# Batch 0's values in rows of 512 bytes, ordered by TensorE, in a fused windowed attention and GELU block

## The chip, the core and the metric

The kernel runs on one core of a Trainium2 chip. Its engines are TensorE (PE, matmuls into PSUM), VectorE (DVE), ScalarE (ACT), GpSimd (POOL) and SyncE (SP, which here only issues transfers); each takes its instructions in order, and they wait for each other by semaphores. The metric is the device time of one execution in microseconds, as the median of several runs. Times inside a run come from one profiled execution.

## The reference

Eight batches of 576 tokens, eight heads of 64. Each token attends to those within 32 places of it; the heads' outputs side by side are the tokens of a two-layer network with GELU (tanh form). All inputs and the output are float32.

```python
scores = np.matmul(q, k.transpose(0, 1, 3, 2)) / np.sqrt(64)          # 8 x 8 x 576 x 576
scores = np.where(np.abs(pos[:, None] - pos[None, :]) <= 32, scores, -1e9)
attn = np.exp(scores - max); attn = attn / (attn.sum(-1) + 1e-9)
x = np.matmul(attn, v).transpose(0, 2, 1, 3).reshape(4608, 512)
out = gelu_tanh(x @ moe_w_in) @ moe_w_out                             # 512 x 2048, 2048 x 512
```

## The kernel before

The 4608 tokens go through the network in nine tiles of 512. Attention of batch t+1 is woven into the second product of tile t, by plans written by hand (`PLAN_0`, `PLAN_1`, `PLAN`); the order of all instructions of an engine is the order of the program. Only batch 0 has nothing to hide in: its attention is the kernel's beginning, and this is where the change lies.

**Layouts.** The 512 first queries and keys of a batch are loaded with four rows to a partition (row 4p + j in partition p, `qk`, L144), cast to fp16, and turned by TensorE for each of four pairs of heads (`trans_pair`, L378). `trans_out` copies the result out of PSUM: queries stay ordered by (j, p), keys are put back in natural order (L390), so that 64 neighbouring keys are one block. Each pair's `score` (L447) multiplies key blocks with the queries that can see them. For batch 0 the mask is added first, by four matmuls of an identity block `idn` with prepared tiles `bias` (L457); every key row of a block must thus stand in the order that `bias` has. The sum of the exponentials comes from a matmul with `ones` (`sum_up`, L495), its inverse from ACT's Ln and Exp (`invert`, L530 and L531). `times` (L505) multiplies the values, 16 matmuls for a pair; `spread` (L540) scales the result on DVE into `xT`, whose four slices are the contraction dimension of the first product, pair g being slice g.

The values `V` hold 128 natural rows to a chunk: slots 0 to 3 are the chunks, slots 4 to 6 hold the blocks shifted by 64, made from the chunks by two DVE copies (`pair_v`, L225 and L226). A pair's values come by two transfers, one for each head, in rows of one token, 256 bytes (`v_of_pair`, L271); POOL casts them into V (`values`, L844; DVE for the last pair).

**The first product.** Tile 0 has 16 column blocks of 128 (`ffn_in`, L577). Each adds four matmuls, dc 0 to 3, one for each slice of `w_in` and of `xT`. `block_in(ns, *dcs)` issues them slice by slice over several columns: six columns first (`six`), then two, six and two. `w_in` comes in eight transfers of 512 KB (`load_w_in`, L246): x is the half of its columns, dc the slice; `cast_w_in` (L250) casts each in two halves, on two engines.

**Order of loads on SP before**: q and k of batch 0 (the first k and one q from ACT's queue) with the keys' tails; the tails of V (`vt`); pairs 0, 1 and 2 of V; w_in dc 0; head 6 of V; w_in dc 1; head 7; w_in dc 2, dc 3, then its other half; then batch 1's q and k and w_out, in turns. Loads share eight semaphores, so each waits for the landing of the load eight before it.

**Order on TensorE before**, from the third score on: score of pair 2, turning of pair 3's q and k, sum of pair 1, score of pair 3, sum of pair 2, `times` 0 and 1, two spins (matmuls with no use but to keep TensorE running), sum 3, two spins, `times` 2, then dc 0 and dc 1 of six columns, `times` 3, dc 2 and dc 3.

Of the kernel before, what the change touches and what calls it, by code (L numbers as in the profile page):

```python
# [78 lines left out]
def kernel(  # L79
# [9 lines left out]
    nc = tc.nc  # L89
# [36 lines left out]
    band = const.tile([128, 4, 144], FP16, name="band")  # L126
    KTs = [const.tile([128, NPAIR, 512], FP16, name=f"KT{i}") for i in range(2)]
# [9 lines left out]
    def load_early(b):  # L137
# [12 lines left out]
        def vs(*cs):  # L150
            if len(raws[b]) < 4:
                raws[b].append(stage.tile([128, 4, H, 64], FP32, name="vr", tag="stage"))
                raws[b].append(tailp.tile([128, 4, 64], FP32, name="vt", tag="vt"))
# [115 lines left out]
    def v_of_pair(g, hs=(0, 1)):  # L269
        for h in (2 * g + x for x in hs):  # L270
            nc.sync.dma_start(raws[0][3][:, :, h, :], v[0, h, 0:512, :].rearrange("(c p) d -> p c d", p=128))  # L271

    vs(4)
    for g in range(3):
        v_of_pair(g)
    for x in range(2):
        load_w_in(0, x)
        v_of_pair(3, (x,))
# [23 lines left out]

    def blocks(copy, dst, src, r, *pieces):
# [14 lines left out]
    nc.vector.memset(ones, 1.0)  # L318

# [58 lines left out]
    def trans_pair(b, pr, pt, ptk=None, now=True, copy=nc.vector.tensor_copy):  # L378
# [4 lines left out]
        for j in range(4):  # L383
            nc.tensor.transpose(ptk[:, j, :], k16[:, pr, j, :, :], idn)
# [3 lines left out]
    def trans_out(b, pr, pt, ptk, copy=nc.vector.tensor_copy):  # L388
        nc.vector.tensor_copy(QTs[b][:, pr, :, 0:128], pt[:, 0:4, :])
        copy(  # L390
            KTs[b % 2][:, pr, :].rearrange("d (p j) -> d p j", j=4),
            ptk[:, 0:4, :].rearrange("d j p -> d p j"))
# [47 lines left out]
    def work_of(b, g):  # L440
# [4 lines left out]
        return (band[:, :, p0:144], range(NPAIR), TAIL if b else TAIL_0, [(7, p0, 144)], p0, 144 - p0)  # L445

    def score(b, g, pair):  # L447
# [5 lines left out]
        if added:  # L453
            for half in range(2):
                for h in range(2):
                    r0 = 64 * h
# [353 lines left out]
    def sums_of(g):  # L810
        d = pieces("DO"[g % 2], "ps_d")
        sum_up(0, g, d, groups[(0, g)])
        lts[g] = invert(0, g, d)
# [9 lines left out]
    score(0, 0, 0)  # L823
    turn(1)
# [8 lines left out]
    cast_vt(0)  # L833
# [5 lines left out]
    score(0, 3, 1)  # L839
    sums_of(2)  # L840

    def values(g, copy):
        hs = slice(2 * g, 2 * g + 2)
        copy(Vs[0][:, 0:4, hs, :], raws[0][3][:, :, hs, :])  # L844
        pair_v(0, nc.vector.tensor_copy, hs)
# [5 lines left out]
    values(0, nc.gpsimd.tensor_copy)  # L851
# [258 lines left out]
```

## Time and profile before

| what | us |
|---|---|
| median of three runs (lowest, highest) | 297.86 (296.98, 298.21) |
| the profiled execution | 299.54 |
| its span from first to last instruction | 297.8 |
| busy in the span: PE, DVE, ACT, POOL | 285.9, 212.8, 196.4, 89.3 |
| busy from 0 to 20 us: PE, DVE, ACT, POOL | 15.65, 11.06, 13.23, 7.76 |
| start of dc 0, dc 1, dc 2 of the first product | 18.03, 20.43, 22.49 |
| start of its casts of w_in on POOL (x = 0, dc 0 to 3) | 16.88, 19.76, 21.82, 23.02 |

Lines of the timeline read: start, duration (both in us), engine and line, operation, output <- input, shape, count; in brackets the idle time of that engine just before, and what ended it. Where a row has a count above one, its duration spans all of them. Lines of windows read, for each engine, busy microseconds and, in brackets, the number of instructions that started; then the granted TensorE clock, the mean busy share of the 16 transfer engines, and the GB/s that they moved. Lines of the chain read start, duration, who.

### The profile page before, as it was taken

What the parts mean: (1) busy time and instruction counts of PE and PEld (TensorE: products, weight loads), DVE (VectorE), ACT (ScalarE), POOL (GpSimd) and SP (SyncE); (2) the same over time, 40 slices, a digit from 0 to 9 for tenths busy, and PEclk for the clock granted to TensorE, in tenths of its full rate; (3) what the DMA queues carried; (4) which work ended last, traced back from release to release, by engine and by line L of the source; (5) the groups of instructions that cost most, each with busy time, mean ns of one, the idle gap of its engine ahead of it and who ended that gap; (6) DMA issues with size and microseconds to landing.
All of it is one profiled execution on the core that took longest, in us unless ns stands there. A gap on an engine that the chain in (4) does not pass through costs nothing.

```text
span 297.8 us, 7286 instructions
## 1 busy us (share of the span) xinstructions
PE 285.9 (96%) x2945; PEld 192.6 (65%) x2945; DVE 212.8 (71%) x467; ACT 196.4 (66%) x315; POOL 89.3 (30%) x143
## 2 busy tenths in 40 slices
PE   7879999999999999999999999999999999999992
PEld 3434544557875687568855885588557867877781
DVE  4655378897897667868786878686857867865852
ACT  5965766778577875777667765786578558707700
POOL 3426315102347622305260615060800050024000
PEclk9999999999999999999999999999999999999999
DMA  7999999999999996999988999999693040013013
GB/s 231 235 327 412 353 310 221 257 183 193 268 240 195 262 219 130 146 130 242 163 191 132 251 117 191 111 244 155 118 147 42 2 130 12 2 36 109 0 55 89
DMA packets 114392, 51.02 MB, mean 171 GB/s; under 512 B 98471, under 2 KB 110247, under 8 KB 114102
## 3 DMA queue, kind: packets, MB, share of 16 engines
q1 hardware_dynamic: 89460, 38.67, 61.4%
q0 software_dynamic: 23776, 10.83, 23.3%
q10 hardware_dynamic: 1122, 1.06, 1.1%
q8 instruction: 23, 0.38, 0.6%
q14 instruction: 11, 0.09, 0.1%
HBM read 36.70 MB, written 9.44 MB: 155 GB/s over the span
## 4 chain that ended last, share of the span: by engine, by line
PE 85%; DMA 6%; SPq 3%; DVE 2%; ACT 1%; issue 0%; POOL 0%; ACTq 0%
PE mm L751 33%; PE ph L577 17%; PE mm L577 17%; PE ps_s L468 3%; PE pu L629 3%; DMA wst<-in_moe_w_in_dram 2%; PE ps_d L495 2%; DMA KT<-k 2%; PE mm L723 2%; PE py L723 2%; PE ps_o L505 2%; SPq L271 2%; DMA qr<-in_q_dram 1%; PE mm L629 1%; PE ps_od L495 1%; SPq L246 1%
## 5 line engine op out<-in xcount | busy, mean ns | idle before, releaser
L577 PEld LDWEIGHTS <-w_in 128*128 128x128 f16 x512 | 57.4, 113 | 50.4 <-POOL w_in L250 2.1
L577 PE MATMUL ph<-xT,w_in 128*128 128x512 f16 x256 | 64.6, 379 | 1.1 <-POOL w_in L250 1.1
L577 PE MATMUL mm<-xT,w_in 128*128 128x512 f16 x256 | 64.1, 379 | 0.0
L713 POOL DMA_DIRECT2D out_dram<-y x55 | 32.3, 597 | 84.9 <-DVE y L780 76.2
L585 ACT ACTIVATE gT<-mm 128x512 f16<-128x512 f32 x60 | 35.6, 598 | 33.1 <-PE mm L577 32.5
L751 PEld LDWEIGHTS <-s 128*128 128x128 f16 x512 | 49.3, 98 | 7.1 <-DVE s L694 0.6
L751 PE MATMUL mm<-t,s 128*128 128x256 f16 x376 | 45.2, 273 | 0.2 <-DVE y L764 0.2
L694 DVE TENSOR_TENSOR s<-gT 128x512 f16<-128x512 f16 x64 | 27.8, 435 | 19.4 <-ACT gT L585 19.3
L751 PEld LDWEIGHTS <-gT 128*128 128x128 f16 x384 | 36.2, 98 | 6.4
L585 ACT ACTIVATE gT<-ph 128x512 f16<-128x512 f32 x58 | 32.4, 604 | 11.2 <-PE ph L577 11.2
L481 ACT ACTIVATE pe<-ps_s 128x960 f16<-128x960 f32 (+1 forms) x31 | 29.6, 976 | 13.4 <-PE ps_s L468 13.3
L751 PE MATMUL mm<-w_out,gT 128*128 128x256 f16 x256 | 32.6, 273 | 0.0
L104 ACT ACT_TABLE_LOAD x18 | 23.1, 1283 | 2.2 <-issue 1.9
L530 ACT ACTIVATE lt<-ps_d 128x480 f32<-128x480 f32 (+2 forms) x28 | 15.5, 555 | 11.4 <-PE ps_d L495 7.9
L531 ACT ACTIVATE lt<-lt 128x480 f32<-128x480 f32 (+3 forms) x36 | 21.1, 586 | 1.1
L490 DVE TENSOR_TENSOR pe<-pe,band 128x960 f16<-128x960 f16 x28 | 18.1, 664 | 2.1 <-ACT pe L481 2.0
L505 PEld LDWEIGHTS <-V 128*64 128x64 f16 x520 | 13.8, 111 | 6.4 <-DVE V L226 1.6
L751 PE MATMUL mm<-t,gT 128*128 128x256 f16 x128 | 16.2, 273 | 0.0
L216 POOL DMA_DIRECT2D V<-in_v_dram x16 | 14.4, 910 | 1.3 <-POOL after L989 0.4
L694 DVE TENSOR_TENSOR s<-s,gT 128x512 f16<-128x512 f16 x32 | 13.9, 435 | 1.1
L751 PE MATMUL mm<-w_out,s 128*128 128x256 f16 x120 | 14.6, 273 | 0.0
L540 DVE TENSOR_TENSOR xT<-ps_o,lt 128x480 f16<-128x480 f32 (+5 forms) x26 | 13.4, 535 | 1.6 <-ACT w_in L250 1.1
(149 smaller groups left out, 390.7 us busy)
## 6 DMA issues: line engine op xcount, KB each, us to landing
kr<-in_k_dram SPq DMA_DIRECT2D x31, 256.0 KB, 9.7
qr<-in_q_dram SPq DMA_DIRECT2D x6, 1024.0 KB, 6.1
wst<-in_moe_w_in_dram SPq DMA_DIRECT2D x8, 512.0 KB, 7.4
wst<-in_moe_w_out_dram SPq DMA_DIRECT2D x2, 1024.0 KB, 10.6
wst<-in_moe_w_out_dram SPq DMA_DIRECT2D x4, 512.0 KB, 7.5
qr<-in_v_dram SPq DMA_DIRECT2D x8, 256.0 KB, 6.9
V<-in_v_dram POOLq DMA_DIRECT2D x16, 128.0 KB, 8.5
qr<-in_q_dram SPq DMA_DIRECT2D x7, 256.0 KB, 7.3
```

What stands on the lines that cost most here:

```text
L104: nc.scalar.add_instruction(mybir.InstLoadActFuncSet(name=nc.get_next_instruction_name(), act_func_set_id=which, ins=[], outs=[]))
L216: nc.gpsimd.dma_start(V[:, c, :, :], v[b, :, 128 * c:128 * c + 128, :].rearrange("h p d -> p h d"))
L481: nc.scalar.activation(pe, ps[:, :, 0:w], AF.Exp, scale=SCALE)
L490: nc.vector.tensor_tensor(pe, pe, m.rearrange("k (o j) p -> k o j p", o=1).broadcast_to(list(pe.shape)), op=ALU.mult)
L505: nc.tensor.matmul(o[64 * h:64 * h + 64, cols].rearrange("d (j p) -> d j p", j=4)[:, :, p0 - q0:p1 - q0], Vs[b % 2][:, slot, 2 * pr + h, : ...
L530: nc.scalar.activation(lt[:, 0:n], d[:, 0:n], AF.Ln)
L531: nc.scalar.activation(lt[:, 0:n], lt[:, 0:n], AF.Exp, scale=-1.0)
L577: nc.tensor.matmul(ph, w_cols[:, dc, fc // 4, fc % 4, :], xT[:, dc, t * 512 % RING:t * 512 % RING + 512], start=(dc == 0), stop=(dc == 3))
L585: nc.scalar.activation(gTs[t][:, fc, :], phs[fc], AF.Gelu_apprx_tanh)
L694: nc.vector.tensor_tensor(dst, x, y, op=op)
L713: eng.dma_start(out_v[b, j, q0 + p:q0 + p + e, cols], yo[m:m + e, cols])
L751: nc.tensor.matmul(pys["apart"][:, 0:256] if apart else py[:, blk, :], lhsT, wino[w][:, f, :], start=(new and i % (8 if one else 16) == 0) ...
```

## The change

Three things in the beginning of the kernel, all for batch 0 alone.

- *Values.* A pair's two transfers now split by rows instead of heads: 256 rows each, two rows to a partition, so that 512 bytes are contiguous. Partition p of half c holds rows 256c + 2p and 2p + 1, which is no chunk of 128 rows. Each pair is cast on POOL into a scratch tile (`v16` in `pad`, which lies in the place of the first tile's `gT`), eight matmuls with 32 columns of a permutation matrix `pick` bring the rows to the partitions where they belong (`turn_pair`), DVE copies the result from PSUM into V (`place_pair`), and `pair_v` follows as before. On SP the order becomes: pair 0, `vt`, pair 1, w_in dc 0, pairs 2 and 3, w_in dc 1, dc 2 and so on.
- *Keys.* `pick` leaves the 64 rows of a block in another order than the natural one, so the keys take the same order: the copy out of PSUM writes them by blocks (`trans_out`), and the mask is added through a permuted identity block (`in_block`), with the natural one for the last eight columns: six matmuls instead of four for each score. The mask that the tail of batch 0 is multiplied with gets its own tile `band_0`, one half of it made by a matmul and an ACT copy.
- *Order.* The four spins go. On TensorE, after the sum of pair 1: turning of V 0, score 3, turning of V 1, sum 2, `times` 0, sum 3, turning of V 2, `times` 1, turning of V 3, dc 0 of six columns, dc 1 of three, `times` 2, dc 1 of the other three, dc 2 of three, `times` 3, dc 2 of the other three, dc 3. On POOL: casts of V 0, `vt`, V 1, V 2, half of w_in dc 0, V 3, then halves of w_in. On DVE: place and pair copies of V 0 and 1, scaling of 0 and 1, place and pair copies of V 2, place of V 3, scaling of 2, pair copies of 3, scaling of 3, half of w_in dc 3, then the copies of `band`. On ACT the other half of w_in dc 0 stands between the inverses of sums 2 and 3.

```diff
+    band_0 = const.tile([128, 4, 16], FP16, name="band_0")
...
-                raws[b].append(stage.tile([128, 4, H, 64], FP32, name="vr", tag="stage"))
+                raws[b].append(stage.tile([128, 4, H, 64] if b else [128, 2, H, 128], FP32, name="vr", tag="stage"))
...
-    def v_of_pair(g, hs=(0, 1)):
-        for h in (2 * g + x for x in hs):
-            nc.sync.dma_start(raws[0][3][:, :, h, :], v[0, h, 0:512, :].rearrange("(c p) d -> p c d", p=128))
-
+    def v_of_pair(g):
+        if len(raws[0]) < 4:
+            vs()
+        for c in range(2):
+            nc.sync.dma_start(raws[0][3][:, c, 2 * g:2 * g + 2, :],
+                              v[0, 2 * g:2 * g + 2, 256 * c:256 * c + 256, :].rearrange("h (p j) d -> p h (j d)", j=2))
+
+    v_of_pair(0)
     vs(4)
-    for g in range(3):
-        v_of_pair(g)
-    for x in range(2):
-        load_w_in(0, x)
-        v_of_pair(3, (x,))
+    v_of_pair(1)
+    load_w_in(0, 0)
+    v_of_pair(2)
+    v_of_pair(3)
+    load_w_in(0, 1)
...
+    pad = gp.tile([128, NF, 512], FP16, name="gT", tag="gT")
+    v16 = pad[:, 0:4, :].rearrange("p g (c h x) -> p g c h x", c=2, h=2)
+    pick = pad[:, 4, 0:128]
+    def in_block(r):
+        return pad[r, 4, 384:448]
+    nc.gpsimd.tensor_copy(pick.rearrange("p (q y a) -> p q y a", q=4, y=2),
+                          idn.rearrange("p (q a y) -> p q y a", q=4, y=2))
+    for r in (even, odd):
+        nc.gpsimd.tensor_copy(in_block(r).rearrange("k (x y a) -> k x y a", x=2, y=2),
+                              idn[r, r].rearrange("k (a y x) -> k x y a", x=2, y=2))
...
+    nc.gpsimd.tensor_copy(band_0[even, :, :], full[even, :, 16:32])
...
-            nc.tensor.transpose(ptk[:, j, :], k16[:, pr, j, :, :], idn)
+            nc.tensor.transpose(ptk[:, j if b else (0, 2, 1, 3)[j], :], k16[:, pr, j, :, :], idn)
...
+        if b == 0:
+            copy(KTs[0][:, pr, :].rearrange("d (b j p) -> d j b p", b=8, j=4),
+                 ptk[:, 0:4, :].rearrange("d j (b p) -> d j b p", b=8))
+        else:
...
-                    nc.tensor.matmul(sides[h][64 * half:64 * half + 64, :], idn[r0:r0 + 64, r0:r0 + 64],
-                                     bias[half][r0:r0 + 64, :, :], start=True, stop=False,
-                                     skip_group_check=True)
+                    for by, cols in (((in_block(r), slice(0, 128)),) if half else
+                                     ((in_block(r), slice(0, 120)), (idn[r, r], slice(120, 128)))):
+                        nc.tensor.matmul(side[:, :, cols], by, bias[half][r, :, cols], start=(cols.start == 0),
+                                         stop=False, skip_group_check=True)
...
+    def cast_pair(g, copy):
+        copy(v16[:, g, :, :, :], raws[0][3][:, :, 2 * g:2 * g + 2, :])
+    def turn_pair(g, ps):
+        at = ps.rearrange("k (c y h d) -> k y c h d", c=2, y=2, h=2)
+        for y in range(2):
+            for half in range(2):
+                for j in range(2):
+                    p0, q0 = 64 * half + 32 * j, 64 * y + 32 * half
+                    nc.tensor.matmul(at[p0:p0 + 32, y, :, :, :], pick[:, q0:q0 + 32],
+                                     v16[:, g, :, :, 64 * j:64 * j + 64], start=True, stop=True)
+    def place_pair(g, ps):
+        nc.vector.tensor_copy(Vs[0][:, 0:4, 2 * g:2 * g + 2, :],
+                              ps.rearrange("k (c h d) -> k c h d", c=4, h=2))
...
-    finish(0, bank(0))
-    finish(1, bank(1))
-    s0 = psS.tile([128, 2, 512], FP32, name="ps_o", tag="S0")
-    spin(2, 512, s0[:, 1, :])
-    sums_of(3)
-    spin(2, 512, s0[:, 1, :])
-    values(2, nc.gpsimd.tensor_copy)
+    cast_pair(0, nc.gpsimd.tensor_copy)
+    cast_vt(0)
+    at0 = psO.tile([128, 512], FP32, name="ps_v", tag="D")
+    turn_pair(0, at0)
+    score(0, 3, 1)
+    place_pair(0, at0)
+    pair_of(0, nc.vector.tensor_copy)
+    cast_pair(1, nc.gpsimd.tensor_copy)
+    at1 = psM.tile([128, 512], FP32, name="ps_v", tag="x1")
+    turn_pair(1, at1)
+    sums_of(2)
+    place_pair(1, at1)
+    pair_of(1, nc.vector.tensor_copy)
+    finish(0, bank(0))
+    cast_pair(2, nc.gpsimd.tensor_copy)
+    nc.gpsimd.tensor_copy(w_in16[:, 0, 0:512], wi[0, 0][:, 0, 0:512])
+    cast_pair(3, nc.gpsimd.tensor_copy)
+    sums_of(3, nc.scalar.copy)
+    at23 = psS.tile([128, 2, 512], FP32, name="ps_v", tag="S1")
+    turn_pair(2, at23[:, 0, :])
+    finish(1, bank(1))
+    turn_pair(3, at23[:, 1, :])
+    place_pair(2, at23[:, 0, :])
+    pair_of(2, nc.vector.tensor_copy)
+    place_pair(3, at23[:, 1, :])
...
-    cast_w_in(0, 0, nc.gpsimd.tensor_copy, nc.scalar.copy)
-    values(3, nc.vector.tensor_copy)
-    block_in(six, 0)
+    block_in((4, 5, 0, 2, 3, 1), 0)
     cast_w_in(0, 1, nc.gpsimd.tensor_copy, nc.scalar.copy)
-    block_in(six, 1)
+    block_in((0, 2, 3), 1)
+    finish(2, s1[:, 0, :])
+    pair_of(3, nc.vector.tensor_copy)
+    block_in((1, 4, 5), 1)
+    cast_w_in(0, 2, nc.gpsimd.tensor_copy, nc.scalar.copy)
+    load_table(gelu_set)
+    block_in((0, 1, 2), 2)
     finish(3, s1[:, 1, :])
-    load_table(gelu_set)
-    cast_w_in(0, 2, nc.gpsimd.tensor_copy, nc.scalar.copy)
+    block_in((3, 4, 5), 2)
     cast_w_in(0, 3, nc.gpsimd.tensor_copy, nc.vector.tensor_copy)
-    block_in(six, 2, 3)
+    block_in(six, 3)
```

More of the change, by code (lines that the diff above doesn't have):

```diff
@@ L389, in trans_out @@
         nc.vector.tensor_copy(QTs[b][:, pr, :, 0:128], pt[:, 0:4, :])
-        copy(
-            KTs[b % 2][:, pr, :].rearrange("d (p j) -> d p j", j=4),
-            ptk[:, 0:4, :].rearrange("d j p -> d p j"))
+        if b == 0:
+            copy(KTs[0][:, pr, :].rearrange("d (b j p) -> d j b p", b=8, j=4),
+                 ptk[:, 0:4, :].rearrange("d j (b p) -> d j b p", b=8))
+        else:
+            copy(
+                KTs[b % 2][:, pr, :].rearrange("d (p j) -> d p j", j=4),
+                ptk[:, 0:4, :].rearrange("d j p -> d p j"))
     def bank(i):
@@ L444, in work_of @@
         p0 = cut(b)
-        return (band[:, :, p0:144], range(NPAIR), TAIL if b else TAIL_0, [(7, p0, 144)], p0, 144 - p0)
+        return (band[:, :, p0:144] if b else band_0, range(NPAIR), TAIL if b else TAIL_0, [(7, p0, 144)], p0, 144 - p0)
     def score(b, g, pair):
@@ L455, in score @@
                 for h in range(2):
-                    r0 = 64 * h
-                    nc.tensor.matmul(sides[h][64 * half:64 * half + 64, :], idn[r0:r0 + 64, r0:r0 + 64],
-                                     bias[half][r0:r0 + 64, :, :], start=True, stop=False,
-                                     skip_group_check=True)
+                    r = slice(64 * h, 64 * h + 64)
+                    side = sides[h][64 * half:64 * half + 64, :].rearrange("k (j p) -> k j p", j=4)
+                    for by, cols in (((in_block(r), slice(0, 128)),) if half else
+                                     ((in_block(r), slice(0, 120)), (idn[r, r], slice(120, 128)))):
+                        nc.tensor.matmul(side[:, :, cols], by, bias[half][r, :, cols], start=(cols.start == 0),
+                                         stop=False, skip_group_check=True)
         for r, pr in enumerate(prs):
@@ L808, with sums_of @@
     lts, os = {}, {}
-    def sums_of(g):
+    def sums_of(g, first=None):
         d = pieces("DO"[g % 2], "ps_d")
         sum_up(0, g, d, groups[(0, g)])
+        if first:
+            first(w_in16[:, 0, 512:1024], wi[0, 0][:, 0, 512:1024])
         lts[g] = invert(0, g, d)
@@ L823 @@
     score(0, 0, 0)
+    ps = psS.tile([128, 2, 512], FP32, name="ps_b", tag="S1")
+    nc.tensor.matmul(ps[odd, 0, 0:64], in_block(odd), full[odd, :, 48:64], start=True, stop=True)
+    nc.scalar.copy(band_0[odd, :, :], ps[odd, 0, 0:64].rearrange("k (j p) -> k j p", j=4))
     turn(1)
@@ L832 @@
     trans_out(0, 2, *pts[2])
-    cast_vt(0)
     spin(1)
@@ L838, with pair_of @@
     sums_of(1)
[L839 to L845, printed above, removed]
+    def cast_pair(g, copy):
[11 more added lines that the diff above has]
+                              ps.rearrange("k (c h d) -> k c h d", c=4, h=2))
+    def pair_of(g, copy):
+        pair_v(0, copy, slice(2 * g, 2 * g + 2))
     def finish(g, o):
@@ L849, in finish @@
         spread(0, g, o, lts[g])
-    values(0, nc.gpsimd.tensor_copy)
-    values(1, nc.gpsimd.tensor_copy)
+    cast_pair(0, nc.gpsimd.tensor_copy)
[23 more added lines that the diff above has]
+    place_pair(3, at23[:, 1, :])
     qk, tails, vs = load_early(1)
@@ L857 @@
     qk(2)
-    finish(0, bank(0))
-    finish(1, bank(1))
-    s0 = psS.tile([128, 2, 512], FP32, name="ps_o", tag="S0")
-    spin(2, 512, s0[:, 1, :])
-    sums_of(3)
-    spin(2, 512, s0[:, 1, :])
-    values(2, nc.gpsimd.tensor_copy)
     s1 = psS.tile([128, 2, 512], FP32, name="ps_o", tag="S1")
-    finish(2, s1[:, 0, :])
     six = range(6)
```

## The prediction, made before the result was known

> **What bounds the kernel now.** I read the page first (its row of TensorE in 40 slices), then the chain of work that ended last, then the first 26 us by windows and as a timeline, since the change touches nothing later except by moving it. The page:
>
> ```profile
> PE 285.9 (96%) x2945; PEld 192.6 (65%) x2945; DVE 212.8 (71%) x467; ACT 196.4 (66%) x315; POOL 89.3 (30%) x143
> PE   7879999999999999999999999999999999999992
> ```
>
> TensorE bounds the span, and only its first three slices (22 us) are not full. So the question is when the full stretch begins. The chain, in order of time, shows on what it waits:
>
> ```profile
> 14.32 7.44 DMA wst<-in_moe_w_in_dram
> 21.82 0.63 POOL w_in L250
> 22.49 0.62 PE ph L577 x2
> ```
>
> The third slice of w_in (dc 2) lands at 21.8, is cast, and the first product goes on at 22.49; its fourth slice costs one more small wait (weights at 23.95, after the POOL cast that starts at 23.02). From there the matmuls of L577 follow each other at 0.216 us until 33 us. I therefore measure the change by one point: the start of dc 3 of columns 0 to 5, **23.95 us** before. Whatever that moves, the end should move. The windows show the transfers that lead to it:
>
> ```profile
> core 0: us, PE busy (x) PEld busy (x) DVE busy (x) ACT busy (x) POOL busy (x), PEclk, DMA share, GB/s
> 7.00:8.00 1.00, 1.00 (x30) 0.77 (x23) 0.17 (x1) 0.70 (x2) 0.61 (x1) 1.00 1.10 356
> 9.00:13.00 4.00, 3.79 (x87) 2.25 (x87) 2.67 (x7) 3.90 (x6) 2.18 (x5) 1.00 1.30 219
> 13.00:14.00 1.00, 0.83 (x26) 0.42 (x18) 0.47 (x2) 1.00 (x2) 0.07 (x1) 1.00 0.37 106
> 14.00:20.00 6.00, 4.02 (x44) 1.75 (x44) 3.73 (x7) 3.46 (x7) 2.10 (x4) 1.00 0.96 289
> 20.00:26.00 6.00, 5.37 (x38) 2.66 (x39) 4.54 (x13) 3.85 (x7) 2.90 (x5) 1.00 1.02 409
> ```
>
> The last two columns: the transfer engines are full (share about 1) but move 219 GB/s while V comes in rows of 256 B, 356 while q and k come in rows of 1 KB, 409 with rows of 4 KB. Between 13 and 14 they are nearly idle (0.37). The prices come from the timeline:
>
> ```profile
> 10.52 0.61 POOL L335 CAST k<-kr 128x512 f16<-128x512 f32 x1 [1.29 <-DMA kr<-in_k_dram]
> 11.18 1.60 SPq L246 DMA_DIRECT2D wst<-in_moe_w_in_dram  x1
> 11.68 0.41 PE L495 MATMUL ps_d<-pe,ones 128*64 128x512 f16 x2
> 13.20 0.28 DVE L226 COPY V<-V 64x384 f16<-64x384 f16 x1
> 14.88 0.60 DVE L226 COPY V<-V 64x384 f16<-64x384 f16 x1
> 15.86 0.60 PE L288 MATMUL ps_o<-KT 128*128 128x512 f16 x2
> 16.88 0.64 POOL L250 CAST w_in<-wst 128x512 f16<-128x512 f32 x1 [1.53 <-DMA wst<-in_moe_w_in_dram]
> 20.26 0.43 DVE L844 CAST V<-vr 128x512 f16<-128x512 f32 x1 [1.36 <-DMA vr<-in_v_dram]
> 21.85 0.44 PE L505 MATMUL ps_o<-pe,V 128*64 128x96 f16 x16
> 22.40 0.69 DVE L540 TENSOR_TENSOR xT<-ps_o,lt 128x512 f16<-128x512 f32 x1 [1.07 <-ACT w_in L250]
> ```
>
> An idle time that a DMA ended dates that landing: the last keys 10.5, w_in dc 0 16.9, the last head of V 20.3.
>
> **The change, part by part.**
>
> *Transfers.* V (1 MB) costs 4.8 us at 219 GB/s. Rows of 512 B are not in the trace: between no gain and the 356 of the 1 KB rows (3.0 us). I take 3.6 us, 0.9 per pair, as both neighbours are one doubling away. The eight issues stay eight (V rows took SP 0.43 to 1.14 us each); each waits for the load eight before it, and by the old landings that holds none back for more than half a microsecond. Counting on from the last keys at 10.5 (vt 128 KB at 219 GB/s 0.6, half a MB of w_in at 409 GB/s 1.3): V pair 0 11.4, vt 12.0, pair 1 12.9, dc 0 14.2, pair 2 15.1, pair 3 **16.0**, dc 1 17.3, dc 2 18.6, dc 3 19.9. The same count for the old order gives dc 2 at 19.8, and the trace 21.8: 2.0 us are lost there, much of it in the empty window 13 to 14 behind SP's issue of 1.60 us. So bounds for pair 3 are 16.0 and 18.0; I take 16.0, since half as many rows stand in the queue when SP comes to that issue.
>
> Trainium skill, "DMA: Bandwidth & Descriptors", Specifications: from 512 B on a transfer runs at line rate. By that, an estimate from the page, V would take the 409 GB/s of the last window, 2.6 us, and every landing from pair 3 on would be a microsecond earlier; no row of 512 B here shows it.
>
> *Set-up.* Four POOL copies (`pick`, two blocks, half of `band_0`): at 0.2 to 0.42 us each (MEMSET and AFFINE_SELECT, L298, L294) at most 1.7, in POOL's wait of 1.96 us for the first keys (before 4.57). One matmul and one ACT copy for `band_0`, at most the 0.37 of the KL copy, in ACT's wait of 0.49 before 9.03. Two more matmuls of 32 columns in each of four scores, between nothing and 0.2 us (L468's two of 32 columns), lie in a stretch where spins fill TensorE. The key copies L390 change their order: between 0.42 (L389, contiguous) and 0.68 as now; three on DVE, off the chain. All at nothing; without cover 0.5 us.
>
> *The new chain for each pair.* Cast on POOL 0.65 (L844: 0.61 to 0.68). Eight TensorE matmuls of 256 columns into 32 output rows: 1.03 if one after the other (8 x 0.108 + 0.17), but the two of 512 columns of L495 take 0.41 where two full-width spins take 0.60, so narrow ones run beside each other; I take 0.40. PSUM copy on DVE 0.69 (L762, L540, f32 from PSUM; below only the 0.42 of L389). Pair copies 0.57 with POOL idle, 0.90 beside a POOL cast (L225 0.29 plus L226 0.28 or 0.60): 0.70. So 1.1 us (turning and PSUM copy) are added between landing and use. The four spins removed (2 x 0.60) stood where TensorE waited anyway.
>
> *The sum.* POOL holds pair 2 (15.1 to 15.75), then half of dc 0 (16.4), then pair 3 (17.05). TensorE takes its instructions in order, so behind pair 3's turning (17.45) stands the whole first product: dc 0, six matmuls 18.75; three of dc 1 19.4; the third pair's product 0.05 + 0.44, 19.9; its scaling on DVE 0.11 + 0.69, 20.7; pair 3's copies on DVE, queued behind it, 21.4; the fourth product 21.9; its scaling 22.7. The rest of dc 1 and dc 2 fits in these waits (dc 2's cast is done by 19.3). dc 3 starts at **22.7**, 1.25 us earlier than 23.95. DVE's own work from 12.6 on (4 x 0.69 + 4 x 0.70 + 4 x 0.69 = 8.3) would end at about 21 without waits, so it is not the bound but near it.
>
> *Later.* w_in's other half lands about 2 us sooner, w_out too (POOL waited for it until 32.52, TensorE needs it at 34.4), so transfers stay ahead of a product that is 1.25 us early. The band copies (1.77 us on DVE) now stand from 23.1 to 24.9, and dc 0 of columns 8 on is needed at about 25.7: still in time, with 0.8 us of slack where there was 1.1.
>
> The profiled execution took 299.54 us, span 297.8 and 1.7 around it: 298.3 after. The median shown is 297.86, 1.7 lower; I forecast the median, 297.86 - 1.25 = **296.6**.
>
> **A rule against it.** Eight spins at the start take 3.27 us, 0.41 each; from 5 us on 0.216. So TensorE has a slow state, although PEclk reads 1.00. The change takes four spins away, and the longest hole that I count is about 1 us (near 15, before pair 2); the old hole of 0.92 us before 20.43 left the next matmuls at 0.216. At the slow rate the twelve matmuls of dc 0 and dc 1 would cost 12 x 0.2 = 2.4 us more; I take nothing. Trainium skill, "TensorE: Matmul & The Clock Gate", Part 1: the clock falls back to half after an idle window of about 3.4 us; by that rule, too, holes of a microsecond cost nothing, but every hole here is nearer to the limit than those of the old order with spins.
>
> **Rivals.**
> 1. *The gain stays in the waits* (297.5): pair 3 lands at 17.0 or POOL's casts stretch to the 0.87 that L250 shows beside DVE; every microsecond there comes one to one out of the 1.25, leaving about 0.3. For it: the 2.0 us lost in the old order. Against: V no longer waits behind dc 1.
> 2. *More than that* (295.5): 512 B rows at the rate of the large ones and pair copies at 0.57: pair 3 at 15.0, dc 3 at 21.6, 2.3 us.
> 3. *Slower* (298.9): DVE becomes the bound. Beside a POOL cast its copies of V cost 0.60 instead of 0.28 (L226; L230's 64x512, 0.59), and POOL now casts nearly without pause from 15 to 21 us. With both halves of all pairs at 0.60 and its eight 128x512 operations at 0.82 (L490's one of that size), DVE has 4 x 1.2 + 8 x 0.82 = 11.4 us of work from 12.6 on, and 1.0 of waits (0.6 between pair 3's copies and its scaling, 0.4 for the second product): dc 3 at 25.0, 1.05 late. It decides from 10.3 us of such work on (23.95 - 1.0 - 12.6); by the rows that I took it is 8.3. For it: DVE has every pair's copies and scalings in one queue. Against: POOL waits for landings in between, and the PSUM reads showed 0.69 beside POOL, too.
>
> **How the numbers follow.** Forecast 0.53 (own range 295.8 to 297.2), rival 1 0.20, rival 2 0.15, rival 3 0.12. A measurement here tells about 0.5%, 1.5 us, from no change: 296.4 and 299.3. Below 296.4: rival 2 and 0.23 of the forecast, 0.38. Above 299.3: half of rival 3, 0.06. Within: 0.56. The range 295.2 to 298.5 leaves out the far halves of rivals 2 and 3.
>
> **What would show it.** Right: V's casts on POOL at about 11.4, 12.9, 15.1 and 16.4; over 250 GB/s from 9 to 13 us and no empty window; PSUM copies of 0.69; the product at 17.5; dc 3 at 22.7, and L577 without holes after. Wrong: turning matmuls at 1.0 us, DVE full from 13 to 23, a product at 0.43 per matmul, or holes after 33 us that take the gain back.

## The result, and the profile after

The changed kernel takes **300.06 us** (299.53 to 300.45, six executions) where the kernel before takes 297.56 (296.43 to 298.78, six executions, the three shown ahead among them): ratio 1.0079, interval 1.0051 to 1.0106. It is slower; the forecast was 296.6. This ratio and those below leave out executions that were over 1.5% longer than the fastest of their kernel, so they are not quite the quotients of the medians.

The profiled execution took 300.22 us with a span of 298.2 (before: 299.54 and 297.8). The point that the prediction measures, the start of dc 3 of columns 0 to 5, came at **25.33 us** instead of 23.95. The page's first part and two of its rows in 40 slices (each 7.5 us):

```profile
PE 287.0 (96%) x2982; PEld 193.5 (65%) x2982; DVE 213.6 (72%) x470; ACT 196.4 (66%) x316; POOL 89.8 (30%) x148
PE   7869999999999999999999999999999999999993
PEclk9979999999999999999999999999999999999999
```

TensorE is still full from the fourth slice on. New is the 7 in the third place of the granted clock: between 15 and 22 us TensorE ran part of the time at a lower rate. The same windows as before (the last three columns are granted clock, share of the transfer engines, GB/s):

```profile
9.00:13.00 4.00, 4.00 (x101) 2.57 (x99) 2.29 (x6) 3.67 (x7) 2.32 (x6) 1.00 1.16 298
13.00:14.00 1.00, 0.60 (x20) 0.35 (x12) 0.90 (x4) 1.00 (x2) 0.43 (x1) 1.00 1.11 334
14.00:20.00 6.00, 3.54 (x56) 1.76 (x53) 3.66 (x8) 4.20 (x8) 2.70 (x5) 0.83 1.05 365
20.00:26.00 6.00, 5.83 (x52) 2.65 (x51) 3.67 (x9) 1.70 (x3) 2.72 (x5) 0.89 1.05 402
```

The transfers did what was foreseen: 298 GB/s where there were 219, and no empty window (334 where there were 106). Yet from 14 to 20 us TensorE is busy for 3.54 us, where it was 4.02. The chain of work that ended last, in its early part, says what stood there:

```profile
10.51 5.70 DMA vr<-in_v_dram
...
16.32 0.61 POOL gT L871
...
17.44 0.62 POOL gT L871
...
18.11 0.62 PE ps_v L879 x8
18.73 1.40 PE ph L603 x3
...
25.33 0.59 PE ph L603 x2
```

The end now hangs on V, not on w_in: the transfers of pair 2 until 16.2, POOL's casts of pairs 2 and 3, the turning of pair 3, and then the first product, whose first three matmuls take 1.40 us, 0.43 from one start to the next instead of 0.216. Two groups of the timeline show the step before it, and two narrower windows the clock:

```profile
16.32 0.61 POOL L871 CAST gT<-vr 128x512 f16<-128x512 f32 x1 [2.90 <-DMA vr<-in_v_dram]
16.99 0.40 PE L879 MATMUL ps_v<-gT 128*32 128x256 f16 x8 [2.10 <-POOL gT L871]
```

```profile
15.00:17.00 2.00, 0.01 (x3) 0.01 (x3) 0.84 (x2) 1.97 (x4) 0.68 (x2) 1.00 1.04 364
18.00:21.00 3.00, 2.90 (x14) 1.04 (x14) 2.74 (x5) 1.99 (x3) 1.37 (x4) 0.50 1.02 412
```

TensorE does nothing from 14.89 to 16.99 while it waits for pair 2; from 17.91 to 21.32 its granted clock is 0.50, for 3.41 us (the trace's own record of the clock has these two times). Later nothing is given back: every tile of the second product starts 1.1 to 1.4 us later than in the trace of before.

### The profile page after: what moved, and what is told of

Its sections match the earlier page's. It is cut to its first block, busy times and chain, and to the rows that moved or that the text cites. A ratio compares the mean times of both kernels' runs of the same rounds, so it can differ in the third digit from the quotient of the medians.

```text
span 298.2 us, 7372 instructions
## 1 busy us (share of the span) xinstructions
PE 287.0 (96%) x2982; PEld 193.5 (65%) x2982; DVE 213.6 (72%) x470; ACT 196.4 (66%) x316; POOL 89.8 (30%) x148
## 4 chain that ended last, share of the span: by engine, by line
PE 88%; DMA 5%; DVE 3%; ACT 1%; issue 1%; POOL 0%; ACTq 0%; DVEq 0%; POOLq 0%
PE mm L777 32%; PE ph L603 19%; PE mm L603 19%; DMA vr<-in_v_dram 3%; PE ps_s L494 3%; PE pu L655 3%; PE ps_d L521 2%; PE ps_o L531 2%; PE mm L749 2%; PE py L749 2%; DMA qr<-in_q_dram 1%; PE mm L655 1%; PE ps_od L521 1%; PE py L777 1%; PE ps_od L531 1%
## 5 line engine op out<-in xcount | busy, mean ns | idle before, releaser
L603 PE MATMUL ph<-xT,w_in 128*128 128x512 f16 x256 | 65.3, 383 | 0.2
L720 DVE TENSOR_TENSOR s<-s,gT 128x512 f16<-128x512 f16 x32 | 14.3, 448 | 1.1
L217 POOL DMA_DIRECT2D V<-in_v_dram x16 | 14.3, 909 | 1.2 <-issue 0.6
```

Source lines behind the costliest of these rows:

```text
L217: nc.gpsimd.dma_start(V[:, c, :, :], v[b, :, 128 * c:128 * c + 128, :].rearrange("h p d -> p h d"))
L603: nc.tensor.matmul(ph, w_cols[:, dc, fc // 4, fc % 4, :], xT[:, dc, t * 512 % RING:t * 512 % RING + 512], start=(dc == 0), stop=(dc == 3))
L720: nc.vector.tensor_tensor(dst, x, y, op=op)
```

## The experiments

**Theory.** (1) The hole of 2.1 us, which the four spins of before would have filled in part, lets the clock fall, and that costs about 1.5 us. (2) The rest is an error in the base: the profiled execution of before was late in just this stretch, so that a usual execution had less to win. **Rivals**: the layout itself is slow (turning, copies, transfers); the new order of the engines is; or the loss arises later.

I call it a fall when an execution's mean granted clock is below 0.995: one stretch of 3.41 us at half rate in 298 us gives 0.994. (The clock also goes to 0.50 at the end, some microseconds after the last matmul, where it costs nothing; in the traces that alone takes the mean to 0.996 at the lowest.) In the five groups of runs below, each on a chip of its own, the kernel before showed a fall in 43 of 131 executions; "without a fall" means the others. Each ratio is against the kernel before on the same chip.

| kernel | executions with a fall | median us | ratio to before (interval) |
|---|---|---|---|
| changed, at first | 6 of 6 | 300.06 | 1.0079 (1.0051, 1.0106) |
| changed, again | 8 of 12 | 299.54 | 1.0049 (1.0024, 1.0074) |
| changed + eight spins | 0 of 12 | 298.84 | 1.0000 (0.9970, 1.0031) |
| before without its four spins | 12 of 12 | 299.17 | 1.0035 (1.0003, 1.0067) |
| before + seven spins | 0 of 12 | 298.45 | 1.0002 (0.9972, 1.0031) |
| changed, values first | 0 of 12 | 298.86 | 1.0029 (1.0000, 1.0058) |
| old values, new order | 6 of 6 | 301.12 | 1.0104 (1.0070, 1.0139) |
| old values, new order, eight spins | 0 of 6 | 300.23 | 1.0068 (1.0048, 1.0089) |
| changed, dc 0 in the hole | 1 of 12 | 299.51 | 1.0051 (1.0027, 1.0075) |
| the same, two copies on ACT | 3 of 12 | 299.72 | 1.0048 (1.0020, 1.0077) |
| changed + spins, pairs 2 and 3 not turned | 0 of 12 | 299.05 | 1.0026 (1.0003, 1.0049) |
| changed, product 1 first | 10 of 12 | 300.41 | 1.0077 (1.0045, 1.0110) |
| the same, a PSUM tile for each turning | 9 of 11 | 300.80 | 1.0082 (1.0053, 1.0112) |
| mended order | 5 of 12 | 299.89 | 1.0054 (1.0020, 1.0087) |
| mended order, values first | 1 of 12 | 298.43 | 1.0023 (0.9993, 1.0052) |
| mended order, own PSUM tiles | 0 of 12 | 298.19 | 0.9996 (0.9973, 1.0018) |

### The clock

*The changed kernel with eight spins behind the sums of pair 3:*

```diff
     sums_of(3, nc.scalar.copy)
+    spin(8, 512, psS.tile([128, 2, 512], FP32, name="ps_o", tag="S0")[:, 1, :])
     at23 = psS.tile([128, 2, 512], FP32, name="ps_v", tag="S1")
```

> Eight spins of 512 columns are put into the hole of the changed kernel (TensorE idle 2.1 us from 14.9 to 17.0, between the sum of pair 3 and the turning of pair 2). Theory A, the clock: the changed kernel's trace grants half clock from 17.9 to 21.3 because TensorE did too little before; with the hole filled the granted clock stays at 1.00 over the whole span, the matmuls of the first product start 0.216 us apart instead of 0.43, dc 3 of the first six columns starts near 23.8 instead of 25.3, and the time falls by 1.4 to 1.7 us, to about 298.5. Rival B, the landing: the loss is that pair 2 of V lands at 16.3 and everything queues behind it; spins do not change that, dc 3 stays within 0.4 us of 25.3 and the time within 0.5 us of 300.1.

Not one fall, and the loss against before, its falls included, is gone (1.0000); against the executions of before without a fall (297.51 on that chip) 1.3 us are left. The same two windows of its trace:

```profile
15.00:17.00 2.00, 2.00 (x10) 0.71 (x9) 1.10 (x3) 1.97 (x4) 0.00 (x0) 1.00 1.03 359
18.00:21.00 3.00, 2.65 (x40) 1.49 (x33) 2.21 (x5) 1.14 (x2) 2.04 (x4) 1.00 1.03 418
```

Useless work in the hole (2.00 us busy instead of 0.01) keeps the clock at 1.00, and the first product's matmuls start 0.22 us apart instead of 0.43. The time is what theory A expected. Its dc 3 (23.8) was missed: this trace has it at 24.72, since pair 2 landed only at 17.1 in it.

*The kernel before without its four spins:*

```diff
-    s0 = psS.tile([128, 2, 512], FP32, name="ps_o", tag="S0")
-    spin(2, 512, s0[:, 1, :])
     sums_of(3)
-    spin(2, 512, s0[:, 1, :])
     values(2, nc.gpsimd.tensor_copy)
```

> The kernel before, with its four spins around the sum of pair 3 taken out and nothing else changed. Theory A: these spins keep the clock up; without them TensorE does about 1.2 us less between 14.3 and 17.7, the granted clock falls to half for a stretch of about 3.4 us, and the time rises by 0.7 to 1.7 us over the kernel before (less than in the changed kernel where the transfers hide part of it). Rival B: nothing falls, the spins stand in time that TensorE waits anyway, and the time stays within 0.5 us of the kernel before.

A fall in every execution, eight of them with two stretches (mean clock below 0.990). So the spins, which take 1.2 us of TensorE's time in the trace and looked free, hold the clock. Their removal is a price of the change by itself.

*The kernel before with seven more spins*: two ahead of the product of pair 0, two between the products of pairs 0 and 1, three between dc 0 and dc 1 of the first product.

> The kernel before with seven more spins: two ahead of the product of pair 0, two between the products of pairs 0 and 1 (where the trace of before shows holes of 0.66 and 0.71 us on TensorE), and three between dc 0 and dc 1 of the first product (a hole of 0.92 us). Theory A (the holes of this stretch decide whether TensorE's clock falls to half for 3.41 us, and each fall costs about 1.5 us): no execution shows a fall, where the kernel before shows one in about every third; the median is that of the undisturbed executions of before, 297.5 us, and a ratio of 0.996 to 0.999. Theory B (the fall of the clock comes from something other than TensorE's idle time, as heat or power): falls as often as before, ratio 1.000. Theory C (the spins delay the products behind them): 0.3 to 0.8 us slower than the undisturbed executions.

Theory B falls: no fall in 12, where the same chip's runs of before had 9 in 23. But theory A's time was missed: the median stayed at 298.45, 0.28 above those of before without a fall (298.17), a little less than C's 0.3 to 0.8. A fall cost 0.6 us by the medians of that chip and came in 9 of 23, so the seven spins cost about as much as they saved.

### The base

*The kernel before, with a profile, twice more, and the changed kernel again:*

> The kernel before once more, for a second trace of it. Both theories: granted clock 1.00, dc 3 at 24.0 within 0.5 us, first matmul of the second product at about 34.4.

> The kernel before, once more with a profile. Theory A (the profiled execution that the prediction rests on was a late one): without a fall of the clock, SP's issue of w_in dc 0 takes about 0.5 us and not 1.60, the window from 13 to 14 us isn't empty, dc 3 starts at 22.5 to 23.2 us and not at 23.95, and the span is 295.0 to 296.5 us. Theory B (that execution was a usual one): dc 3 at 23.7 to 24.2 us, span 297.3 to 298.3.

> The changed kernel as it is, once more, beside the next three on one chip. Clock theory: every execution loses a stretch of half clock (granted clock at or below 0.994), the time is 300.1 within 0.5 us, and dc 3 of the first six columns starts at 25.3 within 0.5. If the clock were a chance of the first profile, a part of the executions would show 0.996 or more and be about 1.2 us faster.

The first of them fell into the lower clock for 6.8 us (dc 3 at 25.17, 300.26 us) and tells of the base only that SP's issue of w_in dc 0 took 0.51 us. The second (298.05 us, span 296.1) settles it. Its SP queue, one window and its chain:

```profile
10.97 0.51 SPq L246 DMA_DIRECT2D wst<-in_moe_w_in_dram  x1
```

```profile
13.00:14.00 1.00, 0.99 (x38) 0.70 (x38) 0.54 (x3) 0.97 (x3) 0.70 (x1) 1.00 1.11 304
```

```profile
14.29 6.42 DMA wst<-in_moe_w_in_dram
20.70 0.05 issue
20.76 0.62 POOL w_in L250
...
22.93 0.62 PE ph L577 x2
```

The issue takes 0.51 us and not 1.60, the window from 13 to 14 moves 304 GB/s and not 106, and dc 3 starts at 22.93, a microsecond earlier than in the trace that the prediction was made from. The traces of before without its spins and with more of them show 0.50 and 0.51 us for that issue, 306 and 320 GB/s. The empty window was an accident of one execution, not a property of the old order. The chain has the same form (w_in bounds it), a microsecond earlier.

The changed kernel's second trace happens to be one without a fall (298.22 us, span 296.2):

```profile
16.09 0.61 POOL gT L871
...
17.20 0.63 POOL gT L871
...
17.87 0.40 PE ps_v L879 x8
...
23.61 0.59 PE ph L603 x2
```

At full clock dc 3 stands at 23.61, 0.68 behind the 22.93 of before's second trace. The four executions of the changed kernel without a fall have a median of 298.40, those of before on that chip 297.61: 0.79, about the same. Seven of the eight with a fall, the one of 304.67 left out, have 299.80, so a fall costs 1.4 us. In traces: 25.33 against 23.61, 1.7 us.

### Layout or order

*The old loads (256 B), keys and casts in the new order of all engines, without turning; then the same with the eight spins:*

> The order alone: the kernel before with its values in rows of 256 B, cast straight into place, keys in natural order, but SP, POOL, TensorE, DVE and ACT in the changed kernel's order, and no spins. Theory A: the clock falls in most executions, as no spins stand there, but the chain is shorter by the turning and the PSUM copy of each pair (DVE has 2.8 us less), while V lands about 1 us later: dc 3 at 23 to 24, time 297.5 to 299. Rival, the rows of 512 B are what the new order needs: pair 3 lands at 18.5 or later, dc 3 at 25 or later, time 300 or more.

> The new order of the end of first attention on every engine, with the old loads of V (rows of 256 B), the old keys and no turning, and with eight spins after the sums of pair 3, so that the clock is held. Beside it stands the earlier run of the changed kernel with the same spins (298.84 us, dc 3 at 24.72 in its trace). Theory A (layout and order are worth little either way at full clock, and what decides is when pairs 2 and 3 land): no fall; 298.0 to 298.8 us; the last pair lands 0.5 to 1 us later than with rows of 512 B, but has no turning and no PSUM copy behind it (1.1 us). Theory B (the new order itself is what costs, as TensorE takes everything behind pair 3): over 299.0 us. Theory C (the layout is what costs): at most 297.6 us, as fast as the undisturbed executions of before.

Without spins a fall in all six executions. With spins and no fall 300.23 us, 2.1 above the executions of before without a fall on that chip (298.17); the changed kernel with the same spins was 1.3 above its own (298.84 against 297.51). So the **layout is worth some 0.7 us in this order** and not a loss, and the **order costs about 2 us with the old layout** even at full clock (a part of it is the spins' own). The rival "the layout is slow" falls. In both traces of the old layout SP's issue of w_in dc 1 took over 3 us (3.02 and 3.15), and dc 3 came at 25.04 and 24.55; whether the old rows in the new order bring this about is not shown, and it is part of these 2 us.

*The loads of pairs 2 and 3 ahead of w_in dc 0, their casts likewise:*

> The changed kernel with the loads of pairs 2 and 3 of V ahead of w_in dc 0 on SP, and POOL's cast of pair 3 ahead of its half of dc 0; no spins. Theory A: pair 2 lands about 1 us earlier, the hole on TensorE shrinks to about 1 us, and whether the clock falls depends on what is left of it: if it holds, as with spins, about 298.5; if it falls, dc 3 still comes 0.3 to 1 us later than with spins. Rival B: the hole itself is the loss; the time falls by about 1 us whatever the clock does.

No fall, and POOL casts pair 2 at 14.76 instead of 16.09 to 16.32, which ends the hole earlier; dc 3 at 23.26. But the trace lost 1.36 us from the second product of the second tile to that of the third (32.31 us instead of 30.95), and the median is 298.86. A loss of 0.5 to 1.4 us between two tiles stands in five other traces too, at three different tiles, two of them traces of the kernel before, so it spreads the times of every kernel. In three of the five TensorE waits 0.53 to 1.26 us for a later batch's keys, loaded by transfers that transpose; whether some versions meet such losses oftener than others was not tried.

### Mending the order

*Four of dc 0's matmuls into the hole, with POOL's half of dc 0 cast first; then also the copies of pairs 2 and 3 out of PSUM on ACT:*

```diff
+    for n in (0, 2, 4, 5):
+        ffn_in(0, n, 0, 1, then=False)
     at23 = psS.tile([128, 2, 512], FP32, name="ps_v", tag="S1")
...
-    block_in((4, 5, 0, 2, 3, 1), 0)
+    block_in((3, 1), 0)
```

> The changed kernel without spins, with work moved into the hole: POOL casts its half of w_in dc 0 before pair 2 of V (dc 0 landed at 13.9 and 14.8 in the two traces, pair 2 at 16.2 and 17.1), and four of the six dc 0 matmuls stand before the turning of pair 2. Theory A, two causes (the clock, and a chain that starts at pair 3's landing near 17 and needs some 6.8 us to dc 3): the clock holds (0.996 or more), the four matmuls start at about 16, dc 3 starts at about 23.8 since DVE's queue (place, copies, scaling) now decides, and the time is 298.2 to 298.7, as with spins or a little under it. Rival, the clock alone: with the clock held and 0.9 us of TensorE work gone from the path behind pair 3, the time falls below 297.8.

> As the run before it, with the copies of pairs 2 and 3 out of PSUM on ACT (idle there, about 0.6 us each) instead of DVE. Theory A: DVE's queue is the chain behind pair 3, so taking 1.4 us from it brings dc 3 forward by 0.7 to 1.2 us, to about 22.8, and the time to 297.2 to 297.8. Rival: TensorE's order or the landings decide and not DVE; the time stays within 0.3 us of the run before it.

dc 0 started at 15.71 and the falls became fewer (1 of 12, 3 of 12), but dc 3 came at 23.49 in the first: work was put into the hole, yet pair 2 stayed late, and the rest of TensorE's queue stood behind it as before. ACT instead of DVE helped no more. Both expectations were missed: even without a fall the medians are 299.38 and 299.63, a microsecond above the 298.40 of the changed kernel on that chip. A loss of 1.26 us at 133 us in the first trace is all that the record shows of where it lies.

*The last two pairs cast straight to their place* (it leaves the ordering of their rows out):

> The changed kernel with the eight spins after the sums of pair 3; it leaves out the ordering of the rows of pairs 2 and 3 (no turning on TensorE, no copy out of PSUM on DVE: POOL casts them straight to where the products read them, so the values of these four heads stand in another order than the reference's). Theory A (at full clock the chain behind pair 3's landing sets dc 3: cast, turning, dc 0, third product, scaling, pair copies, fourth product, scaling): the chain loses pair 3's turning (about 0.4 us) and DVE two copies of 0.69 us; dc 3 0.4 to 1.2 us earlier, 297.6 to 298.4 us against 298.84 with them. Theory B (w_in's last slice, landed at 20.9 and cast, sets dc 3): at most 0.3 us earlier, 298.5 to 298.9 us.

dc 3 at 23.28 and 299.05 us, above both expected ranges, with a loss of 1.26 us at 108 us in the trace. The chips differ, though, and beside the executions of before without a fall on its own chip it is 0.9 slower, where the run with spins was 1.3 slower. So taking the turning of pairs 2 and 3 away is worth about 0.45 us, the lower edge of theory A. It isn't what decides.

*The product of pair 1 ahead of pair 2's turning, alone; then with a PSUM tile for each turning:*

```diff
+    finish(1, bank(1))
-    at23 = psS.tile([128, 2, 512], FP32, name="ps_v", tag="S1")
-    turn_pair(2, at23[:, 0, :])
-    finish(1, bank(1))
-    turn_pair(3, at23[:, 1, :])
+    at2 = psS.tile([128, 2, 512], FP32, name="ps_v", tag="S0")[:, 0, :]
+    at3 = psS.tile([128, 2, 512], FP32, name="ps_v", tag="S1")[:, 0, :]
+    turn_pair(2, at2)
+    turn_pair(3, at3)
```

> The changed kernel with one move alone: the product of pair 1 ahead of the turning of pair 2 instead of behind it. Theory A (in the changed kernel this product, and its scaling on DVE, stand on the chain behind pair 2's landing): the hole on TensorE is cut by 0.44 us and DVE's chain by up to 0.69 us, so dc 3 0.3 to 0.7 us earlier at full clock, 297.7 to 298.2 us in executions without a fall (298.40 in the changed kernel); falls in some executions still, as the hole stays about 1.5 us. Theory B (DVE's place is not on the chain, as dc 0 stands on TensorE behind pair 3 anyway): no change, 298.3 to 298.6 us without a fall.

> The changed kernel with the product of pair 1 ahead of pair 2's turning, as in an earlier run, and a PSUM tile of its own for each of the two turnings; nothing else is moved. Theory A (DVE's copy of pair 2 waited for pair 3's turning by the shared tile): it starts at about 17.1 to 17.3, right behind pair 2's turning, and not at 18.28; the third product still stands on TensorE behind dc 0 and half of dc 1 (20.1 to 20.3 at full clock), so the end moves by at most 0.3 us: 298.0 to 298.5 us in executions without a fall, and falls in most. Theory B (the copy waits for something else): it stays at about 18.3.

DVE's copy of pair 2 out of PSUM, in the first and in the second:

```profile
18.28 0.69 DVE L883 CAST V<-ps_v 128x512 f16<-128x512 f32 x1 [2.05 <-PE ps_v L879]
```

```profile
17.40 0.69 DVE L883 CAST V<-ps_v 128x512 f16<-128x512 f32 x1 [0.56 <-PE ps_v L879]
```

In the first it starts only behind pair 3's turning (17.83 to 18.23), though pair 2 was turned by 17.11: both halves lie in one tile, and the wait is for the tile. With a tile each it starts behind its own turning (16.95 to 17.35). This is a wait that the diff doesn't show and that I had not seen. It isn't what bounds the changed kernel, though: the end didn't move (dc 3 at 23.80, no fall in that trace), because the third product stands on TensorE behind dc 0 and half of dc 1 anyway.

*All of it together* (product 1 first, dc 0 in the hole, the products around dc 1 instead of inside dc 1 and dc 2), then with values first, then with own tiles:

> The changed kernel with its order mended in the stretch from 14 to 23 us: the product of pair 1 stands ahead of pair 2's turning (it waited behind it, and its scaling of 0.69 us then stood on DVE ahead of pair 2's copies); four of dc 0's matmuls ahead of the turning of pair 2 and two between the turnings; pair 3's copies ahead of the scaling of pair 2; the third and fourth product around dc 1 and not inside dc 1 and dc 2; POOL's half of dc 0 ahead of pair 2's cast. Theory A (at full clock the changed order's chain on TensorE and DVE behind pair 3 costs what the earlier landings save, and so an order without these waits keeps the gain): by the landings of the undisturbed execution of the changed kernel (pairs 2 and 3 at 16.0 and 16.8, w_in dc 3 at 21.0) dc 2 at about 20.8 and dc 3 at 22.0 to 22.3 us, against 22.93 in the kernel before and 23.61 in the changed one; 296.6 to 297.4 us, and no fall of the clock, as dc 0 fills the hole. Theory B (what costs lies in the later course, which every early gain meets again): dc 3 earlier but the median over 298.2.

> The changed kernel with pairs 2 and 3 of V loaded ahead of w_in dc 0, and the same mending: the product of pair 1 ahead of pair 2's turning, both turnings ahead of the whole of dc 0, pair 3's copies ahead of the scaling of pair 2, the third product between dc 0 and dc 1, the fourth between dc 1 and dc 2. Theory A (landings and the chain behind them decide): pair 3 landed 15.5 us in an earlier run of this order of loads, so the attention's chain ends at about 20.7 to 21.3 us and only w_in is waited for; dc 0 at 17.4, dc 3 at 21.7 to 22.4 us; 296.5 to 297.4 us. Theory B (the later course takes it back): the median over 298.2.

```diff
+    finish(1, bank(1))
+    for n in (0, 2, 4, 5):
+        ffn_in(0, n, 0, 1, then=False)
+    at2 = psO.tile([128, 512], FP32, name="ps_v", tag="O")
+    at3 = psM.tile([128, 512], FP32, name="ps_v", tag="x1")
+    turn_pair(2, at2)
+    turn_pair(3, at3)
...
+    pair_of(3, nc.vector.tensor_copy)
+    block_in((1,), 0)
+    finish(2, s1[:, 0, :])
+    block_in((0, 2, 4, 5, 1), 1)
+    block_in((3,), 0, 1)
+    finish(3, s1[:, 1, :])
+    block_in(six, 2)
```

> The mended order of the run before (product of pair 1 and four of dc 0's matmuls ahead of pair 2's turning), with a PSUM tile of its own for each of the last two turnings. In the traces so far both halves share one tile, and DVE's copy of pair 2 out of PSUM begins only behind pair 3's turning (idle 2.05 us, ended by that turning, in the run with product 1 first; 2.07 us in the mended order), and the third product only behind the copy of pair 3. Theory A (this shared tile is the wait that keeps the earlier landings from showing): pair 2's copy starts at about 17.2 and not at 18.3, the third product at 18.5 to 19.0 and not at 20.3, dc 2 at 20.4 to 20.9, dc 3 at 21.7 to 22.3 (before: 22.93), 296.5 to 297.2 us, and no fall of the clock, since the hole of 2.0 us behind the turnings goes. Theory B (w_in's landings bound dc 3 at once): dc 3 at 22.5 to 23.0, 297.3 to 297.8 us. Theory C (the later course takes it back): dc 3 early, and yet over 298.2 us.

The first missed (dc 3 at 23.82): the shared tile made DVE idle for 2.07 us, the third product waited for pair 3's copy, and a new hole of 2.01 us opened, with falls in 5 of 12. The second came to 298.43, over the 296.5 to 297.4 expected. The third, with own tiles, had **no fall in 12 and 298.19 us, ratio 0.9996 (0.9973 to 1.0018)**: clear of the changed kernel's 1.0079, level with the kernel before with its falls, and 0.5 us above its executions without one (297.67). The 296.5 to 297.2 us expected were missed. Its chain from pair 2 on has no transfer left in it:

```profile
17.60 0.36 PE ps_v L879 x8
17.96 0.02 issue
17.98 0.70 DVE V L883
...
19.62 0.40 PE ps_o L531 x14
```

dc 3 starts at 23.28 there: in this chain the turning, DVE's copies and TensorE's own order fill the time that the earlier landings made. No version beat the kernel before.

## Why the prediction was wrong, point by point

Forecast 296.6, measured 300.06: 3.46 us. Three terms make it up, each from one pair of traces or medians: base 1.02 (23.95 against 22.93), landings 0.91 (23.61 against 22.7), clock 1.4 (299.80 against 298.40), together 3.3. Traces of single executions on different chips can't be trusted to a tenth of a microsecond, so that the sum fits so closely is in part luck.

- **The clock: the largest of the three.** "The four spins removed stood where TensorE waited anyway", and "the longest hole that I count is about 1 us; I take nothing". They stood in a wait, and that was their worth. The hole became 2.1 us, as pair 2 came a microsecond late and the spins were gone, and in 14 of 18 executions the clock fell. I had 2.4 us as the price for twelve matmuls at the slow rate; the runs show 1.4, and 3.41 us at half rate can't cost more than 1.7 of matmul time. "PEclk reads 1.00" holds for the start (1.00 from 1 to 4 us, while a spin takes 0.41), but not for a fall, where the column shows 0.50. The Trainium skill, "TensorE: Matmul & The Clock Gate", Part 1, gives an idle window of about 3.4 us as the condition and says that the window runs freely and the effect varies from run to run. The length of the fall, 3.41 us, agrees, and so does the variation. The condition read as a hole of 3.4 us doesn't: 2.1 us were enough, in a window of 3.41 us (14.50 to 17.91) in which TensorE was busy for about a third. I had looked at the longest hole, and that was the mistake: the fixed window counts.

  The traces show where the windows lie, since the clock falls again after the last matmul. In the changed kernel's first trace that is at 297.80, 82 times 3.413 us behind the early fall; in all seven traces with an early fall the two are 81, 82 or 83 such steps apart. In the second trace, which has the same hole (14.70 to 16.75) and no early fall, the clock falls at 295.44, and 82 steps ahead of that a window ends at 15.55, in the middle of the hole. The window of the first trace, then the two of the second, then its end:

```profile
14.50:17.91 3.41, 1.16 (x26) 0.74 (x26) 1.32 (x5) 2.69 (x5) 1.58 (x3) 1.00 1.06 350
```

```profile
12.14:15.55 3.41, 2.14 (x60) 1.34 (x53) 3.13 (x8) 3.35 (x7) 0.91 (x2) 1.00 1.07 340
15.55:18.96 3.41, 1.86 (x36) 1.12 (x36) 1.32 (x2) 2.09 (x4) 2.35 (x4) 1.00 1.02 365
295.00:295.44 0.44, 0.00 (x0) 0.00 (x0) 0.00 (x0) 0.00 (x0) 0.00 (x0) 1.00 0.00 0
295.44:296.20 0.76, 0.00 (x0) 0.00 (x0) 0.00 (x0) 0.00 (x0) 0.00 (x0) 0.50 0.00 0
```

  So the phase of the window explains why the same hole brought a fall in one of these two traces and not in the other. With the windows of all 19 traces laid out so, from 4 to 36 us: TensorE was busy for 1.16 to 2.08 us in the seven at whose end the clock fell, and for 1.79 us or more in all others. Busy time alone doesn't settle those between 1.79 and 2.08.
- **The base.** "I forecast the median, 297.86 - 1.25." The 1.25 was counted against the profiled execution, which was 1.7 above the median. I noted that and subtracted all the same. But its lateness lay in the very stretch that the change rebuilds: dc 3 at 23.95 instead of 22.93, an SP issue of 1.60 us, an empty window. The change was credited with removing what a usual execution doesn't have. The other number of the same paragraph, 298.3 against the execution itself, met what the changed kernel does without a fall (298.22 to 298.53). That is luck: dc 3 came 0.9 us later than forecast, and in that trace what stands behind it took 1.2 us less than in the trace of before.
- **The landings.** Pair 2 was to be cast at 15.1 and pair 3 at 16.4; they were at 16.09 and 17.20 at full clock. The rate was right (298 GB/s from 9 to 13 us, and no empty window). What failed is the count by mean rate: in both traces of the changed kernel the first and the last part of a load land about half a microsecond apart until about 13 us and 2 us apart from then on, and POOL waits for the last. The bound for pair 3 (16.0 to 18.0) held, the value taken was its lower end.
- **The chain behind them was right.** From pair 3's cast to dc 3 I counted 6.3 us; at full clock it was 6.4 (17.20 to 23.61). Turning 0.40, the PSUM copy 0.69, pair copies 0.29 and 0.28, the set-up copies and the two extra matmuls of a score hidden, no holes after dc 3: all as taken. I missed the wait in the shared PSUM tile; TensorE's order hides it here.
- **The rivals.** Rival 3 (slower, by DVE) gave the side but not the mechanism: DVE waits for 2.0 us in the stretch, it isn't full. Rival 1, the gain lost in waits, comes nearest to what happens at full clock, where the loss is larger than it said. Rival 2 needed V at the rate of the large rows, and it moved at 298 GB/s and not 409. No rival had the clock; it was named and priced, and left out of the chances.

At full clock the change costs 0.8 us. Its loads land earlier: POOL casts w_in dc 3 at 21.06 in the changed kernel's second trace and at 22.00 in that of before. But by the chains the kernel before was bound by w_in's last slices, while the new one puts the whole first product behind the last pair of V. With the order mended and the hole filled it is level with the kernel before, that one's falls included.

Open: why the parts of a load spread by 2 us from about 13 us on. In every trace one transfer of instructions (16 KB, 0.9 to 1.3 us on one engine) lies at 11.1 to 14.3 us (15.8 in one), and in those of the changed kernel the spread begins with it; in the run with values first a second one at 21.5 us goes with a second step, from 1.8 to 3.2 us, while in those two the second goes without such a step. That it is the cause was not tried. Nor was the phase of the clock's window varied on purpose.

## What to carry to other kernels

Before subtracting a gain from a median, see whether the profiled execution is late in the stretch that the change touches; if it is, count the gain from a second trace, or from the landings that the queue allows. Work with no use in a wait may hold the clock: before taking it away, add up TensorE's busy time over each stretch of 3.4 us, not the longest hole; here no stretch with more than 2.08 us of it brought a fall. And an earlier landing pays only if what stands behind it in the queues is not made longer: here turning, copies and a fixed order of TensorE took it all.

## What the runs showed of the hardware

- The granted clock falls to 0.50 for 3.41 us, or for 6.83 us, after a window of 3.41 us in which TensorE was busy for 1.16 to 2.08 us. A hole of 2.1 us did it in 14 of 18 executions of the changed kernel. The kernel before had a fall in 43 of 131; in the one of them that was traced, TensorE was busy for 2.08 us of the window ahead, with a hole of 1.04 us at its end.
- A packet of 512 B took 33 ns at the median (9 to 13 us, changed kernel) where one of 256 B took 24 (9 to 13 us, before) and one of 1 KB 48 (6 to 9 us, before): the stretch with V in 512 B rows moved 298 GB/s where that with 256 B rows moved 219.
- SP's issue of a 512 KB load of w_in took between 0.33 and 3.15 us; that of dc 1 alone, over all kernels, between 0.47 and 3.15. The kernel before alone, without a fall of the clock, ranged from 296.7 to 301.1 us.
- Two halves of one PSUM tile are not independent for a reader: its copy started at 18.28, behind the matmuls of the other half, 1.2 us after those of its own half had ended; with a tile each it started at 17.40, right behind its own.
